# A two-stage attention kernel on one core: batch-wise phases replaced by a pipeline over row tiles

## The chip, the core and the metric

The kernel runs on one core of one Trainium2 chip. The core has five engines with instruction streams of their own: TensorE (PE) for matmuls, VectorE (DVE), ScalarE (ACT), GpSimd (POOL) and SyncE (SP), which here issues all DMA transfers. PE writes to PSUM, eight banks of 2 KB per partition; DVE and ACT read it. Everything else lies in SBUF. The metric is the time of one execution in microseconds; lower is better.

## The reference

q, k and v have 4 batches, 8 heads, 768 positions and 64 dimensions. The first stage is an attention in which a row sees the 8 first (global) keys and the 96 keys up to its own (local):

```python
keep = (pos[None, :] < n_global) | ((rel >= 0) & (rel < n_local))
scores = scale * q @ k.T - slopes * dist          # per head
a = softmax(where(keep, scores, -1e9)); x = a @ v
```

Its result, 4 x 768 x 512, goes into four causal attention experts of width 64, of which each row uses the two with the largest gate logits:

```python
q, k, v = x @ wq[e], x @ wk[e], x @ wv[e]
ye = softmax(causal(scale * q @ k.T)) @ v @ wo[e]
out += weight_of_expert_e(x @ w_gate) * ye        # two experts per row
```

## The kernel before, in words

Rows are worked on in tiles of 128; a batch has 6 of them, and there are 4 batches. Three functions are called per batch. `load_batch` loads q, k and v of a batch (three 1.5-MB transfers, smaller ones for the first batch), POOL casts them to fp16 (L211, L223), and PE transposes q and k by head pair (L215, tile `tp`), which DVE copies out of PSUM (L218). `local_attention` computes, per head pair and two key tiles, the bias and the scores (L256 to L268, tile `sps`), exponentials on ACT into `abuf` (L273, L278), then per row tile the values (L288 to L298, tile `zps`), the division on DVE (L302, L304) and the transposes of the result x (L308, L312). `experts` projects a whole batch at once: k and q with matmuls of 384 columns (L346, tile `pps`), v and gate logits per row tile (L356, `vps`); then the choice of two experts (`top_two`), the causal scores in chunks of up to 512 columns (L385) with exponentials (L392) and masks on POOL (L402), and per row tile values (L410), division (L414 to L418), transposes (L422), output matmul (L429, `ops`), copy on ACT (L432) and store (L433).

The matmuls of a head or an expert have 64 rows; those of an even and an odd one lie on the two halves of the PE array. Three PSUM pools have two buffers each: `psS` (two banks per buffer) for scores, `psZ` for values, and `psT` (one bank) shared by all else: `tp`, `xps`, `pps`, `vps`, `ztps`, `ops`. A scheduler orders each engine's instructions from the program's order, its own cost model and the free buffers; the order is then fixed, and each engine takes its instructions strictly in it. At the end a small test of the softmax sums decides whether a slow general path is run; with these inputs it is not.

## Time and profile before

| | |
|---|---|
| runs | 242.56 us median of 3 (238.79 to 244.24) |
| profiled execution | 238.55 us, its span 236.3 us |
| granted PE clock, mean | 0.937 of full speed |
| instructions | 4,629, of them 1,830 matmuls and as many weight loads |
| one weight load (L410, before values) | 101 ns mean |
| transferred | 27.70 MB, 117 GB/s over the span |
| DMA issues | q, k, v 21, weights 5, global values 16, output 24 |

The profile is of one execution. Its page gives each engine's busy time; the chain of waits follows what released what, back from the end; the timeline shows single instructions, neighbours of one kind merged; the windows give busy time by stretch, with the granted clock. Matmul lengths include their run through the array and overlap, so a matmul's length is no measure of how often one can start. The transferred bytes include 27.34 MB in the kernel's own queue; the rest is instructions.

### The profile page before, as it was taken

How to read it: one execution, taken by the hardware profiler on the slowest of the kernel's cores; microseconds unless marked ns; L12 is line 12 of the kernel's file. 1: busy time of each engine (PE TensorE's matmuls, PEld its weight loads, DVE VectorE, ACT ScalarE, POOL GpSimd, SP SyncE). 2: the span in 40 equal slices, each digit the busy share in tenths (PEclk: the TensorE clock that was granted, in tenths of full speed). 3: DMA queues.
4: the chain of work that ended last, by engine and by line, in shares of the span. 5: the costliest groups of instructions: out<-in, count | busy, mean ns of one | idle time of the engine just before them, and what ended most of it. 6: DMA issues, size and time to landing. Idle time of an engine off the chain costs nothing.

```text
span 236.3 us, 4629 instructions
## 1 busy us (share of the span) xinstructions
PE 183.5 (78%) x1830; PEld 101.0 (43%) x1830; DVE 118.5 (50%) x396; ACT 99.2 (42%) x141; POOL 77.6 (33%) x170
## 2 busy tenths in 40 slices
PE   0656698666987999678969999779868997996770
PEld 0222245543442644555434544654425445543430
DVE  7310114854674532787672612887754216867440
ACT  2112444000058687400278398000595792027840
POOL 8542441195643245249045300080142000002400
PEclk9999959977997999999995899999999999999995
DMA  8999697979799492495990420000002300000032
GB/s 156 218 218 208 122 230 160 210 167 225 189 220 181 138 217 94 144 219 133 219 186 12 154 108 0 3 1 3 0 1 92 152 28 0 3 0 0 37 143 101
DMA packets 43356, 27.70 MB, mean 117 GB/s; under 512 B 26176, under 2 KB 40000, under 8 KB 43328
## 3 DMA queue, kind: packets, MB, share of 16 engines
q1 hardware_dynamic: 43328, 27.34, 51.5%
q8 instruction: 16, 0.26, 0.5%
q14 instruction: 12, 0.10, 0.1%
HBM read 21.05 MB, written 6.29 MB: 116 GB/s over the span
## 4 chain that ended last, share of the span: by engine, by line
PE 59%; DVE 13%; ACT 9%; POOL 7%; issue 4%; DMA 4%; SPq 0%; ACTq 0%; POOLq 0%
PE pps L346 10%; PE sps L256 6%; PE sps L268 6%; PE vps L356 5%; PE ops L429 5%; PE sps L385 5%; POOL s L211 5%; PE zps L410 4%; DVE x L304 3%; PE xps L308 3%; ACT a L392 3%; PE tp L215 3%; DMA vf<-in_v_dram 3%; ACT abuf L273 2%; PE zps L298 2%
## 5 line engine op out<-in xcount | busy, mean ns | idle before, releaser
L392 ACT ACTIVATE a<-sps 128x1024 f16<-128x1024 f32 x40 | 38.9, 1026 | 87.1 <-PE sps L385 87.1
L402 POOL TENSOR_SCALAR_AFFINE_SELECT a<-a 128x256 f16<-128x256 f16 x40 | 16.3, 407 | 74.9 <-ACT a L392 74.9
L273 ACT ACTIVATE abuf<-sps 128x892 f16<-128x892 f32 x32 | 28.7, 920 | 28.4 <-PE sps L268 27.9
L385 PE MATMUL sps<-qT,kT 64*128 64x512 f16 (+3 forms) x128 | 22.2, 329 | 7.2 <-ACT a L392 7.1
L215 PE MATMUL tp<-ident,s 128*128 128x128 f16 x192 | 20.0, 256 | 9.3 <-POOL s L211 8.1
L302 DVE RECIPROCAL rinv<-zps 128x4 f32<-128x4 f32 x48 | 8.3, 177 | 33.7 <-PE zps L298 33.7
L256 PE MATMUL sps<-biasT,ident 128*128 128x446 f16 x64 | 20.3, 398 | 4.3 <-ACT abuf L278 2.1
L215 PEld LDWEIGHTS <-s 128*128 128x128 f16 x192 | 14.5, 114 | 19.8 <-POOL s L211 17.1
L218 DVE COPY kT<-tp 128x768 f16<-128x768 f16 x16 | 8.9, 556 | 24.0 <-PE tp L215 23.9
L308 PE MATMUL xps<-ident,x 128*128 128x128 f16 x96 | 13.3, 223 | 9.1 <-DVE x L304 8.8
L268 PE MATMUL sps<-qT,kT 64*128 64x223 f16 x192 | 19.9, 273 | 0.0
L304 DVE TENSOR_TENSOR x<-zps,rinv 128x256 f16<-128x256 f32 x48 | 19.1, 416 | 1.0 <-PE xps L308 0.2
L211 POOL CAST s<-qf 128x768 f16<-128x768 f32 x16 | 13.2, 825 | 17.5 <-PE tp L215 17.5
L298 PE MATMUL zps<-v,abuf 128*128 128x65 f16 x192 | 18.9, 195 | 0.0
L410 PE MATMUL zps<-v,a 128*128 128x65 f16 x320 | 18.2, 200 | 0.3
L432 ACT ACTIVATE osb<-ops 128x512 f32<-128x512 f32 x24 | 14.0, 608 | 8.1 <-DMA out_dram<-osb 3.5
L410 PEld LDWEIGHTS <-a 128*128 128x128 f16 x320 | 14.5, 101 | 6.0 <-issue 2.3
L295 PE MATMUL zps<-v,abuf 128*128 128x65 f16 x160 | 16.4, 193 | 0.0
L429 PE MATMUL ops<-wo,zt 128*128 128x512 f16 x48 | 15.6, 410 | 0.5 <-DVE n_f L628 0.3
L223 POOL CAST v<-vf 128x768 f16<-128x768 f32 x16 | 12.8, 828 | 7.4 <-DMA vf<-in_v_dram 7.4
L278 ACT ACTIVATE abuf<-sps 128x446 f16<-128x446 f32 (+1 forms) x32 | 13.3, 467 | 4.3 <-PE sps L268 4.3
L211 POOL CAST s<-kf 128x768 f16<-128x768 f32 x16 | 13.2, 824 | 5.7 <-DMA kf<-in_k_dram 5.1
(104 smaller groups left out, 300.4 us busy)
## 6 DMA issues: line engine op xcount, KB each, us to landing
out_dram<-osb SPq DMA_DIRECT2D x24, 256.0 KB
qf<-in_q_dram SPq DMA_DIRECT2D x4, 384.0 KB
kf<-in_k_dram SPq DMA_DIRECT2D x4, 384.0 KB
vf<-in_v_dram SPq DMA_DIRECT2D x4, 384.0 KB
w<-in_moe_wq_dram SPq DMA_DIRECT2D x1, 512.0 KB
w<-in_moe_wk_dram SPq DMA_DIRECT2D x1, 512.0 KB
w<-in_moe_wv_dram SPq DMA_DIRECT2D x1, 512.0 KB
w<-in_moe_wo_dram SPq DMA_DIRECT2D x1, 512.0 KB
```

Of the source, the lines that this page charges most:

```text
L211: G.tensor_copy(s16[:, :, :, :], src[:, 2 * p:2 * p + 2, :, :].rearrange("j h ct d -> j ct h d"))
L215: nc.tensor.transpose(tp[:, ct * P:(ct + 1) * P], s16[:, ct, :, :].rearrange("j h d -> j (h d)"), ident[:, :])
L256: mm(s_ps[:, hh, 0:2 * W].rearrange("r (j n) -> r j n", j=2), lhsT=ident[:, :], rhs=bt.unsqueeze(1).to_broadcast([P, 2, W]), start=True, s ...
L268: mm(s_ps[:, hh, j * W:j * W + ws[j]], lhsT=kT[p][r0:r0 + Dh, ci * P:(ci + 1) * P], rhs=qT[p][r0:r0 + Dh, ci * P:ci * P + ws[j]], start=Fa ...
L273: S_.activation(a[:, :, c0:c0 + 2, 0:W], s_ps[:, :, 0:2 * W].rearrange("r h (j n) -> r h j n", j=2), func=Exp, scale=sc1)
L298: mm(z_ps[:, hq, :], lhsT=a[:, h % 2, ri, 0:P], rhs=v16[:, h, ri, :], start=False, stop=True, skip_group_check=True)
L304: V.tensor_tensor(x16[:, :, :], z_ps[:, :, 0:Dh], rinv.unsqueeze(2).to_broadcast([P, HG, Dh]), op=Alu.mult)
L346: mm(p_ps[:, :], lhsT=w[:, ko, ep, :, :].rearrange("r a d -> r (a d)"), rhs=xT[:, ko, c * HS:(c + 1) * HS], start=(ko == 0), stop=(ko == N ...
L385: mm(s_ps[:, e2, at:at + n * P], lhsT=kT2[r0:r0 + Hd, ep, ci * P:(ci + 1) * P], rhs=qT2[r0:r0 + Hd, ep, q0 * P:(q0 + n) * P], start=first, ...
L392: S_.activation(a2s[ep][:, :, c * 4 * P:c * 4 * P + n_all], s_ps[:, :, 0:n_all], func=Exp, scale=sc2)
L410: mm(z_ps[:, e, :], lhsT=a2(e, ci, ri), rhs=v2[:, ci, e, :], start=(e == 0 and ci == 0), stop=(ci == ri), skip_group_check=True)
L429: mm(o_ps[:, :], lhsT=zt[:, ep, :], rhs=wo16[:, ep, :], start=(ep == 0), stop=(ep == NEP - 1))
```

## The change

The three functions per batch are replaced by six stages per unit, a unit being one row tile of one batch (24 units). A loop over steps calls, in step s, the causal values of unit s-8, the causal scores of unit s-6, the projections of unit s-5, the local values of unit s-4, global scores of three units at a time, the local scores of unit s-1 and the load and transposes of unit s (`prep`). The weights are loaded in step 1. q, k and v come in 256-KB transfers, one each per unit, with four buffers each. Local scores are now computed per row tile over its own and the previous key tile; projections and causal scores have 128 columns per matmul. `top_two` works on 3 row tiles instead of 6. The PSUM pools and the general path are the same.

```diff
+    raw = fast.enter_context(tc.tile_pool(name="raw", bufs=4))
+    pp = fast.enter_context(tc.tile_pool(name="pp", bufs=3))
...
+    NA = 4
...
+    def prep(u):
+        b, ri = divmod(u, NT)
+        f = {}
+        for nm, src in (("k", k), ("q", q), ("v", v)):
+            f[nm] = raw.tile([P, H, Dh], F32, name=nm + "f")
+            dma(f[nm][:, :, :],
+                src[b, :, ri * P:(ri + 1) * P, :].rearrange("h j d -> j h d"))
+        tp = psT.tile([P, 2, NP, P], F16, name="tp", tag="t")
+        for i, nm in enumerate("kq"):
+            s16 = pp.tile([P, H, Dh], F16, name="s16", tag="s16", bufs=4)
+            G.tensor_copy(s16[:, :, :], f[nm][:, :, :])
             for p in range(NP):
+                nc.tensor.transpose(tp[:, i, p, :],
+                                    s16[:, 2 * p:2 * p + 2, :].rearrange("j h d -> j (h d)"),
+                                    ident[:, :])
+        qk[u] = pp.tile([P, 2, NP, P], F16, name="qkT", bufs=7)
+        V.tensor_copy(qk[u][:, :, :, :], tp[:, :, :, :])
...
+        for t in range(NH):
+            for p in range(NP):
+                mm(g_ps[32 * p:32 * p + 32, t * P:(t + 1) * P],
+                   lhsT=kg[:, p, :, :].rearrange("r a g -> r (a g)"),
+                   rhs=qk[u0 + t][:, 1, p, :], start=(r0 != 0 and t == 0),
...
+        for g in range(NP // 2):
+            s_ps = psS.tile([P, 2, 2, 2 * P], F32, name="sps", tag="s")
+            for hh in range(2):
+                flat = s_ps[:, hh, :, :].rearrange("r a n -> r (a n)")
+                mm(flat[:, 0:2 * w].rearrange("r (a n) -> r a n", a=2),
+                   lhsT=ident[:, :], rhs=biasT[:, hh, 2 * g:2 * g + 2, 0:w],
+                   start=True, stop=False, skip_group_check=True)
+            for i in range(2):
+                p = 2 * g + i
+                for prev in range(2 if ri else 1):
+                    n = NL - 1 if prev else P
+                    at = i * w + prev * P
                     for hh in range(2):
+                        r = slice(hh * Dh, hh * Dh + Dh)
+                        mm(s_ps[:, hh, :, :].rearrange("r a n -> r (a n)")[:, at:at + n],
+                           lhsT=qk[u - prev][r, 0, p, :], rhs=qk[u][r, 1, p, 0:n],
                            start=False, stop=True, skip_group_check=True)
...
+            S_.activation(a[:, :, 2 * g:2 * g + 2, 0:w],
+                          s_ps[:, :, :, :].rearrange("r h a n -> r h (a n)")[:, :, 0:2 * w]
+                          .rearrange("r h (a n) -> r h a n", a=2), func=Exp, scale=sc1)
...
+        x_ps = psT.tile([P, NK, P], F16, name="xps", tag="t")
+        for hf in range(2):
+            z_ps = psZ.tile([P, HG, VW], F32, name="zps", tag="z")
+            mm(z_ps[:, :, :], lhsT=ag[:, c:c + P], rhs=vg[:, hf * HG:(hf + 1) * HG, :],
+               start=True, stop=False, skip_group_check=True)
+            for hq in range(HG):
+                h = hf * HG + hq
+                for prev in range(2 if ri else 1):
+                    mm(z_ps[:, hq, :], lhsT=a[:, h % 2, h // 2, prev * P:(prev + 1) * P],
+                       rhs=vs[u - prev][:, h, :], start=False, stop=True,
...
+    def project(u):
+        b, ri = divmod(u, NT)
+        xT = xTs[u]
+        p_ps = psT.tile([P, 2, NEP, P], F32, name="pps", tag="t")
+        for i, w in enumerate((wk16, wq16)):
+            for ep in range(NEP):
+                for ko in range(NK):
+                    mm(p_ps[:, i, ep, :], lhsT=w[:, ko, ep, :, :].rearrange("r a d -> r (a d)"),
+                       rhs=xT[:, ko, :], start=(i == 0 and ep == 0 and ko == 0),
+                       stop=(ko == NK - 1), skip_group_check=True)
...
+        v_ps = psT.tile([P, E * Hd + E], F32, name="vps", tag="t")
+        for ko in range(NK):
+            mm(v_ps[:, :], lhsT=xT[:, ko, :], rhs=wvg16[:, ko, :],
+               start=(ko == 0), stop=(ko == NK - 1))
...
+        if ri % NH == NH - 1:
+            g = u // NH
+            wts[g] = pp.tile([P, NH, E], F32, name="wt")
+            top_two(pp, lgs[g], wts[g], "", NH)
...
+        b, ri = divmod(u, NT)
+        n = ri + 1
+        a2 = a2s[u] = pp.tile([P, 2, NEP * NT, P], F16, name="a2")
+        blocks = [(ep, ci) for ep in range(NEP) for ci in range(n)]
+        for c0 in range(0, len(blocks), 4):
+            part = blocks[c0:c0 + 4]
+            s_ps = psS.tile([P, 2, 4, P], F32, name="cps", tag="s")
+            for i, (ep, ci) in enumerate(part):
+                for e2 in range(2):
+                    r = slice(e2 * Hd, e2 * Hd + Hd)
+                    mm(s_ps[:, e2, i, :], lhsT=k2s[b * NT + ci][r, 0, ep, :],
+                       rhs=q2s[u][r, 1, ep, :], start=(i == 0), stop=True,
+                       skip_group_check=True)
+            S_.activation(a2[:, :, c0:c0 + len(part), :], s_ps[:, :, 0:len(part), :],
+                          func=Exp, scale=sc2)
+        for e2 in range(2):
+            d = a2[:, e2, 0:NEP * n, :].rearrange("r (p c) q -> r p c q", p=NEP)[:, :, ri, :]
+            G.affine_select(out=d, in_=d, pattern=[[0, NEP], [1, P]],
+                            channel_multiplier=-1, base=0, compare_op=Alu.is_ge, fill=0.0)
...
+        z_ps = psZ.tile([P, E, VW], F32, name="zps", tag="z")
+        for e in range(E):
+            for ci in range(n):
+                mm(z_ps[:, e, :], lhsT=a2[:, e % 2, (e // 2) * n + ci, :],
+                   rhs=v2s[b * NT + ci][:, e, :], start=(e == 0 and ci == 0), stop=True,
+                   skip_group_check=True)
...
-    t = load_batch(0)
-    load_weights()
-    for b in range(B):
-        xT = local_attention(b, t)
-        if b + 1 < B:
-            t = load_batch(b + 1)
-        experts(b, xT)
+    L_SCORES, L_GLOBAL, L_VALUES, L_PROJECT, L_CSCORES, L_CVALUES = 1, 3, 4, 5, 6, 8
+    for s in range(NU + L_CVALUES):
+        for lag, stage in ((L_CVALUES, causal_values), (L_CSCORES, causal_scores),
+                           (L_PROJECT, project), (L_VALUES, local_values)):
+            if 0 <= s - lag < NU:
+                stage(s - lag)
+        if s >= L_GLOBAL and (s - L_GLOBAL) % NH == 0 and (s - L_GLOBAL) < NU:
+            global_scores((s - L_GLOBAL) // NH)
+        if 0 <= s - L_SCORES < NU:
+            local_scores(s - L_SCORES)
+        if s < NU:
+            prep(s)
+        if s == 1:
+            load_weights()
```

On PE, at the end of one batch's projections, the order before goes from `pps` to `vps`, with the first causal scores between them:

```order
L346 MATMUL pps<-xT,wq_121 128x384
L346 LDWEIGHTS wq_121
L385 LDWEIGHTS kT_2305
L385 MATMUL sps<-qT_2304,kT_2305 128x512
L356 LDWEIGHTS xT
L356 MATMUL vps<-wvg_123,xT 128x260
```

In the changed kernel, in the middle of the run, the values of one unit (`zps`, from buffers of earlier units) are followed by the output matmul of another and the projections of a third:

```order
L343 LDWEIGHTS a_1003
L343 MATMUL zps<-v_586,a_1003 128x65
L343 MATMUL zps<-v_734,a_1003 128x65
L362 LDWEIGHTS zt
L362 MATMUL ops<-wo_129,zt 128x512
L293 LDWEIGHTS wk_127
L293 MATMUL pps<-xT,wk_127 128x128
```

So neighbours on PE now belong to different units. On SP the order before has the loads of the last batch, then the remaining outputs (the row with x14):

```order
L433 DMA out_dram<-osb 128x512 x2
L192 DMA vf<-in_v_dram 128x48x64
L192 DMA kf<-in_k_dram 128x48x64
L192 DMA qf<-in_q_dram 128x48x64
L198 DMA vgf<-in_v_dram 16x1x64 x2
L433 DMA out_dram<-osb 128x512 x2
L198 DMA vgf<-in_v_dram 16x1x64 x2
L433 DMA out_dram<-osb 128x512 x14
```

The changed order has three loads of later units between two output stores:

```order
L177 DMA qf<-in_q_dram 128x8x64
L177 DMA vf<-in_v_dram 128x8x64
L197 DMA vgf<-in_v_dram 16x1x64 x4
L177 DMA kf<-in_k_dram 128x8x64
L366 DMA out_dram<-osb 128x512
L177 DMA qf<-in_q_dram 128x8x64
L177 DMA vf<-in_v_dram 128x8x64
L177 DMA kf<-in_k_dram 128x8x64
L177 DMA qf<-in_q_dram 128x8x64
L366 DMA out_dram<-osb 128x512
L177 DMA vf<-in_v_dram 128x8x64
```

Each store of `osb` now has loads queued behind it. On DVE the order before copies all `pps` of a batch and then the `vps`:

```order
L218 COPY kT<-tp 128x768
L218 COPY qT<-tp 128x768
L349 CAST kT_1521<-pps 128x384 x2
L349 CAST qT_1520<-pps 128x384 x2
L358 CAST v_1570<-vps 128x4x64
L360 COPY lg<-vps 128x4
```

In the changed order one unit's copies out of the shared `psT` tiles stand between division steps of other units:

```order
L297 CAST kq_3099<-pps 128x512
L305 CAST v_3106<-vps 128x4x64
L308 COPY lg<-vps 128x4
L283 COPY xT<-xps 128x512
L188 COPY qkT<-tp 128x1024
L347 RECIPROCAL rinv_125<-zps 128x4
L349 TENSOR_TENSOR ce<-rinv_125,wt 128x4
L351 TENSOR_TENSOR zs<-zps,ce 128x256
L359 COPY zt<-ztps 128x256
L274 RECIPROCAL rinv_124<-zps 128x4
L276 TENSOR_TENSOR x_3318<-zps,rinv_124 128x256
```

One round of these rows is one unit's share of DVE's work, apart from the choice of experts.

## Rows read from the trace of the kernel before

**Rows 1.** The page, busy us of each engine, share, instructions.
```profile
PE 183.5 (78%) x1830; PEld 101.0 (43%) x1830; DVE 118.5 (50%) x396; ACT 99.2 (42%) x141; POOL 77.6 (33%) x170
```

**Rows 2.** Timeline of PE: start, length in us, engine, line, operation, count merged.
```profile
108.27 0.51 PE L215 MATMUL tp<-ident,s 128*128 128x128 f16 x6 [0.26 <-POOL s L211]
108.72 1.51 PE L346 MATMUL pps<-xT,wk 128*128 128x384 f16 x8
...
190.48 0.54 PE L256 MATMUL sps<-biasT,ident 128*128 128x446 f16 x2
190.96 0.37 PE L268 MATMUL sps<-qT,kT 64*128 64x223 f16 x4
191.26 0.56 PE L256 MATMUL sps<-biasT,ident 128*128 128x446 f16 x2
...
225.22 0.49 PE L410 MATMUL zps<-v,a 128*128 128x65 f16 x11
```

**Rows 3.** Chain of waits: start, length in us, what; first projections of each batch.
```profile
57.31 5.48 PE pps L346 x24
...
108.77 4.38 PE pps L346 x24
...
159.11 4.38 PE pps L346 x24
...
204.03 3.87 PE pps L346 x20
```

**Rows 4.** Windows: busy us of PE, PEld, DVE, ACT, POOL; clock, DMA share, GB/s.
```profile
7.00:57.00 50.00, 34.16 (x309) 19.52 (x309) 16.55 (x43) 11.39 (x17) 23.17 (x49) 0.89 1.02 193
10.00:20.00 10.00, 5.66 (x33) 2.50 (x33) 1.11 (x2) 2.65 (x4) 4.20 (x6) 1.00 1.35 218
57.00:69.50 12.50, 12.50 (x72) 6.25 (x71) 7.78 (x21) 2.18 (x3) 6.08 (x10) 0.89 0.92 208
69.50:80.00 10.50, 7.97 (x82) 3.50 (x82) 5.33 (x26) 9.42 (x13) 4.26 (x13) 0.84 0.67 136
80.00:101.00 21.00, 18.86 (x236) 10.57 (x236) 9.17 (x31) 12.58 (x21) 7.01 (x12) 1.00 0.62 172
101.00:108.70 7.70, 5.42 (x80) 4.17 (x77) 6.29 (x15) 0.00 (x0) 4.90 (x9) 1.00 0.72 148
119.80:131.00 11.20, 8.67 (x80) 4.05 (x79) 5.40 (x25) 9.34 (x12) 5.56 (x12) 0.71 0.45 108
```

**Rows 5.** Waits: who waited for whom, us in total, times, longest.
```profile
ACT a L392 <- PE sps L385: 87.1, 15, 26.2
...
PE sps L385 <- ACT a L392: 7.1, 12, 0.6
```

**Rows 6.** Instructions by line and shape: count, busy us, mean ns, idle before.
```profile
L392 ACT ACTIVATE a<-sps 128x1024 f16<-128x1024 f32 x40 | 38.9, 1026 | 87.1 <-PE sps L385 87.1
L273 ACT ACTIVATE abuf<-sps 128x892 f16<-128x892 f32 x32 | 28.7, 920 | 28.4 <-PE sps L268 27.9
...
L211 POOL CAST s<-qf 128x768 f16<-128x768 f32 x16 | 13.2, 825 | 17.5 <-PE tp L215 17.5
...
L349 DVE CAST qT<-pps 128x384 f16<-128x384 f32 x16 | 8.9, 557 | 3.8 <-PE pps L346 3.0
L218 DVE COPY qT<-tp 128x768 f16<-128x768 f16 x16 | 8.9, 557 | 5.7 <-PE tp L215 5.1
...
L331 DVE TENSOR_TENSOR el<-el,ge 128x24 f32<-128x24 f32 x4 | 1.5, 366 | 2.2 <-ACT el L330 2.2
...
L322 DVE TENSOR_TENSOR ge<-lg,m 128x24 f32<-128x24 f32 x4 | 0.6, 158 | 0.0
```

**Rows 7.** Timeline, the last microseconds.
```profile
226.00 4.62 SPq L433 DMA_DIRECT2D out_dram<-osb  x4
...
229.37 0.60 ACT L432 ACTIVATE osb<-ops 128x512 f32<-128x512 f32 x1 [0.69 <-PE ops L429]
```

**Rows 8.** Waits of SyncE's DMA queue.
```profile
SPq L433 <- ACT osb L432: 119.9, 18, 39.2
```

More of the change, by code (lines that the diff above doesn't have):

```diff
@@ L47 @@
     WP = 2 * P
+    NU = B * NT
+    NH = 3
+    HG = H // 2
     VW = Dh + 1
@@ new lines, in global_scores @@
+    def global_scores(g):
+        u0 = g * NH
+        b, r0 = divmod(u0, NT)
+        kg, _ = gl[b]
+        g_ps = psS.tile([P, NH * P], F32, name="gps", tag="s")
+        if r0 == 0:
+            mm(g_ps[:, 0:P], lhsT=ident[:, :], rhs=gmask[:, :], start=True, stop=False,
+               skip_group_check=True)
+        for t in range(NH):
+            for p in range(NP):
+                mm(g_ps[32 * p:32 * p + 32, t * P:(t + 1) * P],
+                   lhsT=kg[:, p, :, :].rearrange("r a g -> r (a g)"),
+                   rhs=qk[u0 + t][:, 1, p, :], start=(r0 != 0 and t == 0),
+                   stop=True, skip_group_check=True, tile_position=(0, 32 * p))
+        ag = pp.tile([P, NH * P], F16, name="ag", bufs=3)
+        S_.activation(ag[:, :], g_ps[:, :], func=Exp, bias=gbias[:, :], scale=sc1)
+        ags[g] = ag
@@ new lines, in local_scores @@
+    def local_scores(u):
+        ri = u % NT
+        a = abuf[u % NA]
+        w = W if ri else P
+        for g in range(NP // 2):
[10 more added lines that the diff above has]
+                    at = i * w + prev * P
@@ L313, in local_attention, with local_values @@
-        return xT
-    def top_two(pool, lg, wt, nm):
+            S_.activation(a[:, :, 2 * g:2 * g + 2, 0:w],
+                          s_ps[:, :, :, :].rearrange("r h a n -> r h (a n)")[:, :, 0:2 * w]
+                          .rearrange("r h (a n) -> r h a n", a=2), func=Exp, scale=sc1)
+    def local_values(u):
+        b, ri = divmod(u, NT)
+        a, ag, vg = abuf[u % NA], ags[u // NH], gl[b][1]
+        c = (ri % NH) * P
+        x_ps = psT.tile([P, NK, P], F16, name="xps", tag="t")
[8 more added lines that the diff above has]
+                       rhs=vs[u - prev][:, h, :], start=False, stop=True,
+                       skip_group_check=True)
+            rinv = rinv1[:, b, ri, hf * HG:(hf + 1) * HG]
+            V.reciprocal(rinv, z_ps[:, :, Dh])
+            x16 = pp.tile([P, HG, Dh], F16, name="x16")
+            V.tensor_tensor(x16[:, :, :], z_ps[:, :, 0:Dh],
+                            rinv.unsqueeze(2).to_broadcast([P, HG, Dh]), op=Alu.mult)
+            for j in range(2):
+                nc.tensor.transpose(x_ps[:, 2 * hf + j, :],
+                                    x16[:, 2 * j:2 * j + 2, :].rearrange("r h d -> r (h d)"),
+                                    ident[:, :])
+        xTs[u] = pp.tile([P, NK, P], F16, name="xT")
+        V.tensor_copy(xTs[u][:, :, :], x_ps[:, :, :])
@@ new lines, in causal_values @@
+    def causal_values(u):
+        b, ri = divmod(u, NT)
+        n, a2 = ri + 1, a2s[u]
+        z_ps = psZ.tile([P, E, VW], F32, name="zps", tag="z")
[3 more added lines that the diff above has]
+                   rhs=v2s[b * NT + ci][:, e, :], start=(e == 0 and ci == 0), stop=True,
+                   skip_group_check=True)
+        rinv = rinv2[:, b, ri, :]
+        V.reciprocal(rinv, z_ps[:, :, Hd])
+        ce = pp.tile([P, E], F32, name="ce")
+        V.tensor_mul(ce[:, :], rinv, wts[u // NH][:, ri % NH, :])
+        zs = pp.tile([P, E, Hd], F16, name="zs")
+        V.tensor_tensor(zs[:, :, :], z_ps[:, :, 0:Hd],
+                        ce[:, :].unsqueeze(2).to_broadcast([P, E, Hd]), op=Alu.mult)
+        zt_ps = psT.tile([P, NEP, P], F16, name="ztps", tag="t")
+        for ep in range(NEP):
+            nc.tensor.transpose(zt_ps[:, ep, :],
+                                zs[:, 2 * ep:2 * ep + 2, :].rearrange("r e d -> r (e d)"),
+                                ident[:, :])
+        zt = pp.tile([P, NEP, P], F16, name="zt")
+        V.tensor_copy(zt[:, :, :], zt_ps[:, :, :])
+        o_ps = psT.tile([P, D], F32, name="ops", tag="t")
+        for ep in range(NEP):
+            mm(o_ps[:, :], lhsT=zt[:, ep, :], rhs=wo16[:, ep, :],
+               start=(ep == 0), stop=(ep == NEP - 1))
+        o_sb = pp.tile([P, D], F32, name="osb")
+        S_.activation(o_sb[:, :], o_ps[:, :], func=Copy)
+        dma(out[b, ri * P:(ri + 1) * P, :], o_sb[:, :])
@@ L331, in top_two @@
         V.tensor_mul(el[:, :, :], el[:, :, :], ge[:, :, :])
-        z = pool.tile([P, NT], F32, name=nm + "z")
+        z = pool.tile([P, n], F32, name=nm + "z")
         V.reduce_sum(z[:, :], el[:, :, :], axis=Ax.X)
```

310 lines of the change are left out of this document (56 added, 254 removed).

## The prediction

> **What bounds the kernel now.** I read the busy totals first [rows 1]: TensorE (PE) is busy 183.5 of 236.3 us, no other engine over 118.5. So PE is the engine to watch, but a PE that waits between overlapping matmuls also counts as busy, so the next question is what it needs when nothing holds it up.
>
> The timeline of PE answers that [rows 2]. Six transposes of 128 columns with a weight load each take 0.51 us; the last lasts about 0.22, so starts are 58 ns apart. Eight matmuls of 384 columns are (1.51-0.35)/7 = 166 ns apart, eleven of 65 columns (0.49-0.19)/10 = 30 ns. That is 0.43 to 0.46 ns per column whatever the width, with the weight load hidden in every case. Matmuls on 64 rows run in pairs: four of 223 columns end in 0.37 us, of which 0.26 is the last one's own length, so the second pair starts 0.105 us after the first. A change between full-array matmuls and pairs costs more: from the first 446-column bias matmul at 190.48 to the first pair at 190.96 are 0.48 us for 892 columns, which stream in 0.385; from that pair to the next bias matmul are 0.30 us for two pairs (0.21). I take 0.095 us per change.
>
> The program before has 283,600 columns (pairs counted once, the four 32-column strips of the global scores once) and 215 such changes: 283,600 x 0.43 ns = 122 us, plus 20, is 142 us of PE need, 35.5 us per batch. The chain of waits shows the projections of the batches starting at 57.31, 108.77, 159.11 and 204.03 us [rows 3]: a batch takes some 50 us. PE thus uses 0.71 of a batch's time, and the first 57 us serve one batch's first attention only.
>
> Where the rest goes is in the stretches [rows 4]. In the projections (57 to 69.5) PE is never idle, while ScalarE (ACT) works 2.18 of 12.5 us. In the causal scores (69.5 to 80) ACT works 9.42 of 10.5 and PE waits for it. Around the last local values (101 to 108.7) VectorE (DVE) works 6.29 of 7.7 and ACT nothing. In the local scores mixed with causal values (80 to 101) all three have something, and PE is busy 18.86 of 21. ACT's first causal exponentials wait 87.1 us in all for PE, while PE waits 7.1 for ACT [rows 5]: each engine in turn is the limit while the others stand still.
>
> **The change, part by part.** *PE.* The same columns. Projections go from 128 matmuls of 384 columns to 384 of 128, global scores from 32 to 96, local scores from 192 to 352, causal scores from 128 to 336: 656 matmuls and weight loads more, and the instruction order has 226 changes of kind. By the spacing above, 3 x 58 = 174 ns stand for one 166: 128 x 8 ns = 1 us; the others the same or less. With 11 more changes (1 us) PE needs 144 us, 6.0 per unit of 128 rows (24 units). The Trainium skill ("TensorE: Matmul & The Clock Gate", Back-to-back issue gap) gives about 81 ns for sustained matmuls of 128 columns with their weight loads; by it the 384 projections would cost 9 us more, and the total below would be 9 us higher. The transposes at 58 ns speak against it here, so the sum keeps 58.
>
> *DVE.* Copies out of PSUM: 80 before (768 columns in 0.557 us, 384 fp32 in 0.557 [rows 6]), 72 after over the same elements; at most the same time. The choice of two experts is now made 8 times instead of 4, ten instructions of 0.16 to 0.37 us each [rows 6]: 40 more, some 8 us. 118.5 + 8 = 126 us, 5.3 per unit. *ACT:* the same elements; causal exponentials go from 44 to 48 (4 of 1.03 us fewer, 8 half ones more), local ones from 64 to 48 at up to 0.92 [rows 6], global ones and the small ones 4 more each: 99.2 becomes about 102, 4.3 per unit. *GpSimd (POOL):* casts 32 of 0.824 us become 48 over the same elements; with their fixed parts under 90 us, 3.7 per unit. *Transfers:* the same bytes, 0.79 MB in and 0.26 out per unit. The best stretch of only loads moved 218 GB/s [rows 4], so 4.8 us per unit. No engine but PE exceeds 5.3, and in a steady state all work on different units at once.
>
> *Start.* The first output matmul stands in PE's order behind the transposes of 8 units. These need 8 x 0.786 + 2.13 MB of weights = 8.4 MB. At 218 GB/s that is 38.5 us, at the 193 of the stretch 7 to 57, which has the weight loads and their waits for casts in it [rows 4], 43.5; I take 42, near the row with the same kind of traffic. PE's need for everything ahead of this point is 24 us, so loads set it; in the kernel before, only a part of one batch's local attention was done by then.
>
> *Steady part.* PE still needs 144-24 = 120 us. How much of the time will it use? The lower end is 0.73, what the last full period before gives: 44.9 us from 159.11 to 204.03 with a need of 32.8, as it has no loads to transpose. The upper end is 0.90, the mixed stretch 80 to 101, PE busy 18.86 of 21 [rows 4]. The new order is a mixture throughout, but DVE is loaded to 0.72 in it (5.3/6.0 x 0.82) against 0.44 in that stretch, with ACT at 0.6 in both. I take 0.82, midway: 146 us. Ends: 133 and 164.
>
> *Drain.* The last unit's chain from its projection on (three exponentials of 1.03, masks, values, division, output) is about 10 us, and PE has older units' work for part of it: between 0 and 10, I take 5. *Tail.* From the end of the last output copy at 229.97 to the span's end are 6.3 us [rows 7], unchanged. The profiled execution took 238.55, 2.25 outside the span.
>
> Sum: 42 + 146 + 5 + 6.3 + 2.25 = 201.6, taken as **201 us**, against 238.55 for the profiled execution and a median of 242.56 (238.79 to 244.24). What I cost at nothing: extra weight loads (hidden by the matmul ahead; uncovered, the 0.1 us length of each would make 66 us), extra POOL instructions (hidden while POOL is below 6 us per unit).
>
> *Queues passed.* SyncE issues loads and stores in one order. Before, it waits 119.9 us for output copies with nothing behind them that matters [rows 8]. Now loads of later units stand behind each output store: at the first store 8.7 units' loads are issued and the ninth unit's transposes follow soon after, so there a late copy delays a load; at the eleventh store loads are 21 units ahead, three more than are needed, and a delay costs nothing. The few early units may add 3 us each, inside the 0.73 to 0.90.
>
> **Rivals.** (1) *The waits move.* Six tiles per unit (transposes, x, two projections, two output tiles) share two PSUM banks, and each is freed by DVE or ACT. Their own production and copying add to some 7.3 us per unit (0.51+0.7, 1.1+0.4, 0.9+0.7, 0.6+0.6, 0.6, 1.2), 3.7 with two banks; if every reader comes about 1.6 us late, because it queues behind 1-us exponentials or a chain of small DVE instructions, it is 8.4 us per unit, as now. For it: the two are loaded to 0.7 and 0.6 and take their work in a fixed order. Against: between a tile's last matmul and the next use of its bank the new order has another stage. 120/6 = 20 units' work at 8.4 = 168: 42+168+5+8.6 = 224 us, spread 212 to 236.
>
> (2) *Slower: PE drops to 1.2 GHz.* In 119.8 to 131, where PE waited for ACT (busy 9.34 of 11.2 us) between causal pairs, the granted clock was 0.71, in 7 to 57 it was 0.89, in 80 to 101 it was 1.00 [rows 4]. If the steady part has that broken rhythm, its 101 us of streaming can double. Slower than 243.3 (2% over 238.55) needs 40 us more, so 0.4 of the work at the low clock; with 0.6 of it the time is 262. For it: thinner matmuls with many short waits. Against: the mixed stretch kept the full clock at 0.9 busy, and this is the busier kind. The Trainium skill (the same page, A second HAM failure mode) says that a PE made idle again and again by cycling PSUM tiles swings between the two levels; the 0.71 stretch agrees, the mixed one does not.
>
> (3) *Transfers become the bound.* With 256-KB loads and stores alternating, if the rate falls to 130 GB/s, 27.3 MB take 210 us, and with start and tail 222; at 120, 238: no change. For it: loads are requested only as buffers come free. Against: the same packets moved at 208 and 218 GB/s [rows 4], and four units of buffers cover more than 20 us.
>
> **How the numbers follow.** Main case, PE paced: 0.62, 182 to 212. Rival 1: 0.22. Rival 2: 0.09, of it 0.07 slower. Rival 3: 0.07, half of it within 2%. The likeliest gives 201. The range 180 to 228 holds the main case and most of rival 1, and leaves out about 2 in 10. A measurement of this kernel tells about 2% from no change. Faster: 0.62 + 0.20 + 0.04 = 0.86; within 2%: 0.07; slower: 0.07.
>
> **What would show it.** Right: the first output matmul near 42 us; PE busy near 0.9 from then to 185 us without stretches in which ACT or DVE stands still; DVE about 126, ACT about 102 us; PE spacing of 58 ns in the projections; granted clock at 1.00 after the start. Wrong: PE waits for copies of the shared PSUM tiles in every unit (rival 1); long stretches at 0.5 clock (rival 2); casts that wait for loads late in the run (rival 3); projections at 81 ns or more per matmul; a first output matmul after 50 us.

## The result, and the profile after

The changed kernel takes 205.84 us (median of 4 runs, 204.39 to 206.3), against 240.87 for the kernel before in the same comparison: a ratio of 0.861, 95% interval 0.855 to 0.867. The forecast was 201, with 180 to 228 as its range. The profiled execution took 204.39 us, of which the span is 202.7. Some executions, most of them of the kernel before, take over 1.5% longer than its fastest, and ratios here and below leave them out.

The busy totals, answering to [rows 1]: PE's share rises from 78 to 83%. With 656 more matmuls its 168.2 us are still less than the 183.5 before, since time in which PE waits between overlapping matmuls, or streams at a lower clock, counts as busy, and there is less of it (mean granted clock 0.962, before 0.937).

```profile
PE 168.2 (83%) x2486; PEld 116.5 (57%) x2486; DVE 117.0 (58%) x428; ACT 101.9 (50%) x137; POOL 78.5 (39%) x217
```

Five stretches, with the columns of [rows 4]: length, busy us of PE, PEld, DVE, ACT and POOL with counts, clock, DMA share, GB/s.

```profile
0.00:10.00 10.00, 3.49 (x27) 2.16 (x28) 6.09 (x29) 2.37 (x3) 7.29 (x37) 1.00 0.96 180
10.00:36.00 26.00, 17.43 (x185) 9.94 (x184) 7.29 (x21) 5.87 (x7) 13.54 (x44) 0.96 0.94 185
36.00:53.00 17.00, 14.71 (x211) 10.64 (x208) 9.45 (x34) 8.27 (x12) 8.93 (x21) 0.86 0.79 141
53.00:190.00 137.00, 127.91 (x2039) 91.23 (x2035) 91.30 (x333) 82.76 (x112) 47.96 (x116) 1.00 0.57 131
190.00:202.70 12.70, 4.62 (x38) 2.50 (x38) 2.86 (x15) 2.63 (x4) 0.77 (x2) 0.67 0.20 69
```

From 53 to 190 us the mixture is what the forecast hoped for: PE busy 127.91 of 137, DVE at 0.67 and ACT at 0.60 beside it, full clock. The start is where the time is: until 36 us PE is busy 20.9 of 36 us. The output matmuls are one line; its record gives the first and last start:

```profile
L362 PE MATMUL ops<-wo,zt x48: 378/379/632, 53.1 to 196.2; 128*128 128x512 f16 x48
```

53.1 us is 11 later than the forecast's 42. The chain of waits (start, length, what) shows what stands before it:

```profile
10.48 4.66 DMA w<-in_moe_wq_dram
...
15.20 1.33 POOL wq L136 x4
...
16.65 4.34 DMA w<-in_moe_wk_dram
...
21.05 1.44 POOL wk L136 x4
...
22.51 4.44 DMA w<-in_moe_wv_dram
...
27.00 1.44 POOL wvg L141 x4
...
28.86 4.72 DMA qf<-in_q_dram
...
34.38 0.62 PE tp L184 x4
```

The four weight loads share one staging tile (pool `wst`, `bufs=1`), so each waits for POOL's casts of the one before. On SyncE's queue loads of units 2 to 4 stand between them and wait with them; the q in these lines is unit 4's, behind the fourth weight load (issued at 28.45). I had counted the bytes of the weights, not this alternation.

The waits by engine (total, times, longest), answering to [rows 5, 8]:

```profile
POOL a L333 <- ACT a L329: 52.4, 16, 7.3
ACT abuf L253 <- PE sps L250: 50.1, 29, 7.2
...
ACT a L329 <- PE cps L326: 14.7, 20, 2.2
...
PE ztps L355 <- DVE zs L351: 5.8, 10, 1.2
...
PE sps L240 <- ACT a L329: 1.8, 3, 0.6
...
SPq L366 <- ACT osb L365: 96.1, 24, 8.8
```

ACT's causal exponentials waited 87.1 us for PE before, with a longest of 26.2; now 14.7 and 2.2. PE's own waits are small. SyncE still stands 96.1 us before stores, 24 times, now with loads behind it.

PE's timeline around one unit's projections, to be read as [rows 2]:

```profile
101.02 0.61 PE L293 MATMUL pps<-xT,wk 128*128 128x128 f16 x8
101.47 0.61 PE L293 MATMUL pps<-xT,wq 128*128 128x128 f16 x8
101.92 0.61 PE L301 MATMUL vps<-wvg,xT 128*128 128x260 f16 x4
```

Eight matmuls of 128 columns in 0.45 us are 56 ns each, the forecast's 58.

### The profile page after: what moved, and what is told of

Same layout as the page of the kernel before. It is cut to its first block, busy times and chain, and to the rows that moved or that the text cites. A ratio compares the mean times of both kernels' runs of the same rounds, so it can differ in the third digit from the quotient of the medians.

```text
span 202.7 us, 6148 instructions
## 1 busy us (share of the span) xinstructions
PE 168.2 (83%) x2486; PEld 116.5 (57%) x2486; DVE 117.0 (58%) x428; ACT 101.9 (50%) x137; POOL 78.5 (39%) x217
## 4 chain that ended last, share of the span: by engine, by line
PE 59%; DVE 15%; DMA 9%; SPq 5%; ACT 4%; POOL 3%; issue 2%; ACTq 0%; DVEq 0%; POOLq 0%
PE pps L293 11%; PE sps L240 7%; PE ops L362 6%; PE sps L250 6%; PE vps L301 4%; PE tp L184 4%; DVE qkT L188 4%; PE zps L343 4%; PE cps L326 4%; PE xps L279 4%; SPq L177 3%; PE zps L270 3%; PE ztps L355 3%; DVE zs L351 3%; DMA qf<-in_q_dram 2%; DMA w<-in_moe_wq_dram 2%
## 5 line engine op out<-in xcount | busy, mean ns | idle before, releaser
L253 ACT ACTIVATE abuf<-sps 128x892 f16<-128x892 f32 (+1 forms) x48 | 40.2, 862 | 50.3 <-PE sps L250 50.1
L329 ACT ACTIVATE a<-cps 128x1024 f16<-128x1024 f32 (+1 forms) x48 | 42.2, 915 | 15.5 <-PE cps L326 14.7
L297 DVE CAST kq<-pps 128x512 f16<-128x512 f32 x24 | 16.6, 691 | 32.4 <-PE pps L293 32.4
L240 PE MATMUL sps<-biasT,ident 128*128 128x446 f16 (+1 forms) x96 | 29.3, 375 | 3.9 <-ACT a L329 1.8
L188 DVE COPY qkT<-tp 128x1024 f16<-128x1024 f16 x24 | 16.5, 688 | 23.7 <-PE tp L184 22.8
L184 PE MATMUL tp<-ident,s 128*128 128x128 f16 x192 | 18.3, 235 | 10.5 <-POOL s L182 10.3
L182 POOL CAST s<-kf 128x512 f16<-128x512 f32 x24 | 14.8, 619 | 26.0 <-issue 12.2
L250 PE MATMUL sps<-qkT 64*128 64x128 f16 (+1 forms) x352 | 20.4, 226 | 1.3 <-DVE qkT L188 1.3
L270 PE MATMUL zps<-v,abuf 128*128 128x65 f16 x352 | 20.4, 194 | 0.0
L270 PEld LDWEIGHTS <-abuf 128*128 128x128 f16 x352 | 18.0, 98 | 1.7 <-issue 0.4
L191 POOL CAST v<-vf 128x512 f16<-128x512 f32 x24 | 14.7, 614 | 10.8 <-DMA vf<-in_v_dram 10.7
L182 POOL CAST s<-qf 128x512 f16<-128x512 f32 x24 | 14.8, 616 | 8.3 <-DMA qf<-in_q_dram 8.3
L326 PE MATMUL cps<-kq,kq 64*128 64x128 f16 x240 | 14.8, 219 | 0.8 <-ACT a L329 0.6
L293 PE MATMUL pps<-xT,wq 128*128 128x128 f16 x192 | 15.3, 223 | 0.0
```

The lines of the kernel that those rows point to most:

```text
L182: G.tensor_copy(s16[:, :, :], f[nm][:, :, :])
L184: nc.tensor.transpose(tp[:, i, p, :], s16[:, 2 * p:2 * p + 2, :].rearrange("j h d -> j (h d)"), ident[:, :])
L188: V.tensor_copy(qk[u][:, :, :, :], tp[:, :, :, :])
L240: mm(flat[:, 0:2 * w].rearrange("r (a n) -> r a n", a=2), lhsT=ident[:, :], rhs=biasT[:, hh, 2 * g:2 * g + 2, 0:w], start=True, stop=False ...
L250: mm(s_ps[:, hh, :, :].rearrange("r a n -> r (a n)")[:, at:at + n], lhsT=qk[u - prev][r, 0, p, :], rhs=qk[u][r, 1, p, 0:n], start=False, s ...
L253: S_.activation(a[:, :, 2 * g:2 * g + 2, 0:w], s_ps[:, :, :, :].rearrange("r h a n -> r h (a n)")[:, :, 0:2 * w] .rearrange("r h (a n) -> ...
```

## The experiments

Medians are compared with the changed kernel's 205.84 us, which was timed in the first comparison only. The kernel before spreads more (238.7 to 246.5 us over all comparisons), so ratios to it move by a per cent between comparisons, and a difference of a per cent between two experiments decides little. Where idle time of PE or its need ahead of a point is given, it is worked out from all PE rows of that run, the need at the forecast's prices (0.43 ns per column, 0.095 us per change).

### Where the gain comes from: e_nolag and e_phase

e_nolag drops the lags between a unit's stages; with them goes the order within a step, which now begins with the newest unit (`...` marks lines left out):

```diff
-    L_SCORES, L_GLOBAL, L_VALUES, L_PROJECT, L_CSCORES, L_CVALUES = 1, 3, 4, 5, 6, 8
...
+    for s in range(NU + 4):
         if s < NU:
             prep(s)
+            local_scores(s)
...
+        if 2 <= s < NU + 2:
+            for stage in (local_values, project, causal_scores):
+                stage(s - 2)
+        if s >= 4:
+            causal_values(s - 4)
```

> The lags alone undone: the same stages unit by unit, but a unit's local values, projection and causal scores follow one another in one step, and its causal values two steps later; between them stand only the next units' transposes and local scores. Theory A, the lags are what hides each stage's copy or exponential behind another stage's matmuls: a unit shows about 0.5 (division), 0.4 (copy of x), 0.7 (copy of q and k) and half of the exponentials, some 2 us more per unit: 240 to 260 us. Rival B, the order in which each engine's queue is laid out mixes units by itself, so that the written lags matter little: 205 to 215 us.

Measured 244.86 us (243.65 to 245.51), the kernel before 243.94 beside it (238.72 to 246.1): theory A, and the whole gain is gone. The page's row of granted clock (40 slices, tenths), its busy line, and PE's timeline in one unit:

```profile
PE 180.8 (75%) x2486; PEld 131.4 (54%) x2486; DVE 121.4 (50%) x428; ACT 99.7 (41%) x137; POOL 78.0 (32%) x217
...
PEclk9999999769977999569977999569977899569975
```
```profile
121.12 0.28 PE L326 MATMUL cps<-kq,kq 64*128 64x128 f16 x4
122.37 0.34 PE L326 MATMUL cps<-kq,kq 64*128 64x128 f16 x6 [0.97 <-ACT a L329]
...
123.38 0.54 PE L240 MATMUL sps<-biasT,ident 128*128 128x446 f16 x2 [0.61 <-ACT a L329]
...
124.73 1.03 PE L362 MATMUL ops<-wo,zt 128*128 128x512 f16 x2
...
128.78 0.22 PE L219 MATMUL gps<-gmask,ident 128*128 128x128 f16 x1 [0.81 <-ACT abuf L253]
...
130.06 0.28 PE L265 MATMUL zps<-vg,ag 128*128 128x260 f16 x1 [0.78 <-ACT ag L228]
```

Waits of 0.6 to 1.0 us follow one another, and PE drops to half clock (1.2 GHz) for 3.4 to 10.2 us some 27 us apart, 68.9 us in all against 17.3 in the changed kernel: two output matmuls take 1.03 us here and 0.60 there. Of the 39.2 us of span, 26.6 are idle (span less busy: 61.1 against 34.5) and 12.6 more busy time. Matmuls of 128 columns start 107 ns apart at half clock and 56 at full, 0.4 ns more per column. By that the columns streamed at half clock cost some 22 us here, against 4 in the changed kernel; the 106 changes of kind that this order saves (120 against 226) give part of that back. This is the forecast's rival 2, seen in another kernel: the Trainium skill ("TensorE: Matmul & The Clock Gate", A second HAM failure mode: psum-queue depth-cycling) describes a PE that swings between its levels when short idle times come again and again, and this trace agrees. With the lags the steady part shows none of it (clock 1.00). They have a price, though: without them the first output matmul comes at 43.4 us, 9.6 earlier than in the changed kernel; the loss is in the 191.9 us from the first to the last one, against 143.1.

e_phase keeps the lags and undoes the mixing of batches and of the two attentions (with more buffers for q, k, v and x, as that needs):

```diff
-    for s in range(NU + L_CVALUES): ...
+    for b in range(B):
+        ...                       # global_scores; local_scores, local_values 3 behind
+        for s in range(NT):
+            project(u0 + s)
+        for s in range(NT + 2):   # causal_values 2 behind causal_scores; next batch's prep
+            ...
```

> The mixing alone undone: the same tiles, matmuls, copies and stage functions as in the changed kernel, but a batch at a time (six units of local attention with their own lags, six projections, six units of causal attention with the next batch's transposes among them), with enough buffers for that. Theory A, the gain of the change is that ScalarE's, VectorE's and PE's stages of different units overlap: with phases ACT limits causal scores (48 exponentials, 42 us in all), PE the projections, and each phase drains: 225 to 245 us, PE idle or waiting for ACT a at more than 20 us. Rival B, the gain comes from the smaller tiles and the shorter start (one unit instead of one batch before work begins): 203 to 215 us.

Measured 220.38 us (219.44 to 221.32): between the two, neither theory. The first output matmul starts at 64.5 us, 11.4 later than in the changed kernel, and the batches follow every 45 us (64.5, 109.7, 154.5) where units a batch apart follow every 42 (53.1, 95.3, 136.8). In a whole batch PE is busy 0.90:

```profile
66.00:111.30 45.30, 40.99 (x626) 27.89 (x621) 29.78 (x99) 25.32 (x35) 18.45 (x46) 1.00 0.80 168
```

ACT's causal exponentials wait 42.2 us for PE instead of 14.7, so the engines do take turns more, but lags within a phase already cover most of it. Of the 35 us, then, mixing the phases is worth 14.5. The first output matmul's 11.4 us are only in part a loss: by then PE has done more (a need of 29.8 us against 24.2) and been idle 6.0 us longer (23.4 against 17.4). From the first to the last output matmul it's idle 4.7 us longer (15.6 against 10.9), and the order has 30 changes of kind more. The other 20 us come with thin units and lags inside a phase.

### What sets the start: e_wbuf, e_wlate, e_hoist

```diff
-    wst = fast.enter_context(tc.tile_pool(name="wst", bufs=1))
+    wst = fast.enter_context(tc.tile_pool(name="wst", bufs=4))
```

> One size: the staging tile of the weights gets four buffers instead of one, so that no weight load waits for the casts of the one before. Changed kernel: 205.8 us; in its chain the weight loads stand one behind another (4.66, 4.34, 4.44 us, with 1.33, 1.44, 1.44 us of casts between them), and the first output matmul starts at 53.1 us instead of the 42 forecast. Theory A, the chain of weight loads sets the start: four loads and their casts, 22 us, fall to the 2.1 MB's own 10 to 12 us, the first output matmul comes at 43 to 46 us, 196 to 200 us. Rival B, the start is bound by what the DMA engines carry at this packet size (DMA share 0.94 and 185 GB/s from 10 to 36 us): the first output matmul stays at 50 us or later, 203 to 206 us.

Measured 202.29 us (201.99 to 204.44), ratio 0.845 (0.838 to 0.852); first output matmul at 50.4 us. Between the two: loads went from 185 to 217 GB/s, so rival B's limit isn't one, yet the start is B's, since PE stood from 16.9 to 23.1 us: unit 2's q and v were still behind 2.1 MB of weights. PE's idle time before the first output matmul is 17.4 us, as in the changed kernel. What is shorter is its busy time, 33.0 against 35.7 us, with none at half clock where the changed kernel has 6.8 us. So the gain may be the clock's and not the load rate's; no run separates them.

```profile
10.00:36.00 26.00, 16.50 (x196) 10.35 (x195) 7.20 (x19) 6.28 (x8) 14.05 (x41) 1.00 1.18 217
```
```profile
23.11 0.61 PE L184 MATMUL tp<-ident,s 128*128 128x128 f16 x4 [6.17 <-POOL s L182]
```

e_wlate, on top of e_wbuf, moves the weights two units further down:

```diff
-        if s == 1:
+        if s == 3:
             load_weights()
```

> Two places: four staging buffers for the weights as in e_wbuf, and their loads and casts three units into the program (behind unit 3's loads and casts) instead of one. In e_wbuf the first output matmul came at 50.4 us: unit 2's loads stood behind 2.1 MB of weights and PE was idle from 16.9 to 23.1 us, then needed 27 us to get there. Theory A, the 24 us of PE work ahead of the first output matmul stand in series with that wait, and loads by themselves (8.4 MB at the 217 GB/s of e_wbuf, 39 us) do not set it: with the weights behind four units PE works while they land, first output matmul at 42 to 46 us, total 194 to 198 us. Rival B, the projections of unit 0 now wait for weights that come later, and the start stays at 49 to 52 us: 201 to 204 us.

Measured 203.63 us (202.83 to 204.41), first output matmul at 52.2: theory A fell as stated, but rival B's reason was not the one at work either. POOL's timeline shows it:

```profile
24.58 0.13 POOL L190 MEMSET v<- 128x8 f16 x1 [5.30 <-PE zps L270]
27.03 0.13 POOL L190 MEMSET v<- 128x8 f16 x1 [2.32 <-PE zps L270]
27.07 1.43 POOL L136 CAST wq<-w 128x256 f16<-128x256 f32 x4
...
32.32 0.61 POOL L182 CAST s<-kf 128x512 f16<-128x512 f32 x1
```

The MEMSETs of units 7 and 8, placed early in POOL's order, waited for PE to release the v tiles of units 0 and 1, and the weights' casts stood behind them. e_hoist takes away what makes them wait:

```diff
-        vs[u] = pp.tile([P, H, VW], F16, name="v16", bufs=7)
-        G.memset(vs[u][:, :, Dh:VW], 1.0)
+        vs[u] = vbuf[u % NV]      # ring of seven, column of ones set once ahead
```

> One place, on top of e_wlate: the v tiles become a ring of seven buffers whose column of ones is set once, instead of a MEMSET per unit. In e_wlate's trace the MEMSETs of the 7th and 8th next unit stood ahead of the weights' casts on POOL and waited 5.30 and 2.32 us for PE to release unit 0's and 1's tiles, and the casts of unit 4 came only at 32.3 us, with PE idle for 5.46 us. Theory A, POOL's order set that start: all weights have landed by some 26 us, unit 4's first cast comes at 27 to 28 us, first output matmul at 44 to 48 instead of 52.2 us, 196 to 200 us. Rival B, the weights land too late anyway or PE's order holds the start: first output matmul at 50 us or later, 202 to 205 us.

Measured 200.85 us (200.21 to 202.38), ratio 0.837 (0.832 to 0.842); first output matmul at 49.0, just above A's 44 to 48, the total just above its 200. Theory A in its mechanism: the first cast of unit 4 comes at 29.22 instead of 32.32, now waiting for its load alone, and PE's idle time before the first output matmul falls from 17.1 us in e_wlate to 13.6.

```profile
29.22 0.61 POOL L189 CAST s<-kf 128x512 f16<-128x512 f32 x1 [0.25 <-DMA kf<-in_k_dram]
```

One number nearly recurs: from the transposes of unit 4's q, which stands behind weight loads in all of these, to the first output matmul are 53.1 - 34.4 = 18.7 us in the changed kernel, 17.0 in e_wbuf (from 33.4), 17.9 in e_wlate (34.3) and in e_hoist (31.1), for 12.3 to 13.9 us of need. Loads and POOL's order decide when this piece begins (in e_wbuf by way of the long wait at unit 2), PE's work and its clock how long it is: in e_best below it is 21.5 us, 11.3 of them at half clock.

### The price of PE's instructions: e_split and e_group

```diff
-                    mm(p_ps[:, i, ep, :], lhsT=w..., rhs=xT[:, ko, :], ...)
+                    for c in (0, Hd):
+                        mm(p_ps[:, i, ep, c:c + Hd], lhsT=w..., rhs=xT[:, ko, c:c + Hd], ...)
```

> One cost doubled: each of the 384 projection matmuls of 128 columns becomes two of 64 columns with the same weights, 384 matmuls and weight loads more for the same columns. Theory A, a matmul costs its columns (0.43 ns each, 30 ns for the 65 columns of the values) and weight loads are hidden: 0 to 2 us more, 205 to 208 us. Rival B, a matmul with a new weight load has a floor: at the 56 ns of the 128-column ones it is 384 x 56 = 21 us of PE, 222 to 228 us; at the 98 ns of a weight load over 250 us.

Measured 208.09 us (206.98 to 209.71): 2.3 us more, at the edge of A and far from B.

```profile
111.48 0.64 PE L294 MATMUL pps<-xT,wk 128*128 128x64 f16 x16
111.96 0.63 PE L294 MATMUL pps<-xT,wq 128*128 128x64 f16 x16
```

Sixteen matmuls of 64 columns take 0.48 us, eight of 128 took 0.45: 0.03 x 48 such groups is 1.4 us, and weight loads stay hidden at 30 ns a matmul. The forecast's 1 us for its added matmuls stands. The 9 us that it worked out from the Trainium skill's figure for 128 columns ("TensorE: Matmul & The Clock Gate", Back-to-back issue gap) does not show: those matmuls run 56 ns apart here.

e_group emits the bias matmuls of both halves of the local scores before the pairs:

```diff
+        tiles = []
         for g in range(NP // 2):
             s_ps = psS.tile(...)
+            tiles.append(s_ps)
             ...                   # the two bias matmuls
+        for g, s_ps in enumerate(tiles):
             for i in range(2):    # the pairs, the exponential
```

> One part of the order: in the local scores of a unit the bias matmuls of both halves come first and then all pairs, so that PE changes between full-array and 64-row matmuls 48 times less; the work is the same. Theory A, each such change costs 0.095 us of PE, and PE sets the pace: 48 x 0.095 = 4.6 us, at 0.85 use about 5 us less, 200 to 202 us. Rival B, the change costs nothing by itself (the time is the drain of one shape's array use, given back elsewhere) or PE does not set the pace: 204.5 to 206.5 us. Rival C, both tiles of local scores must now be free together before the first pair, and PE waits for the exponentials: 207 to 212 us, with PE's waits for ACT a and abuf grown from 2 to over 10 us.

Measured 204.06 us (203.47 to 204.84), ratio 0.851 (0.845 to 0.856): 1.8 us less, between A and B. The built order changes kind 196 times instead of 226, not 48 times less, so A's own price gives 30 x 0.095 = 3 us. Inconclusive between a part of A and nothing. The price itself can be read from the changed kernel's records: over its 85 changes into pairs and 85 out of them between 53 and 188 us, start to start beyond the columns (0.43 ns each) is 99 and 106 ns on average (worked out from all PE rows of the stretch). The two matmuls of a pair start 3 to 4 ns apart and stream together, so the columns of one are subtracted in full; the 127 ns in e_pool4's expectation below count half of them. The forecast took 95 for both. The Trainium skill ("TensorEngine Tiling (Array Packing)", Key Properties) says that a change of tiling mode drains the engine; that each change costs about 100 ns here agrees.

### Banks and queues: e_psT3, e_pool4, e_order, e_storeq

```diff
-    psZ = ...(tc.tile_pool(name="psZ", bufs=2, space=PSUM))
-    psT = ...(tc.tile_pool(name="psT", bufs=2, space=PSUM))
+    psZ = ...(tc.tile_pool(name="psZ", bufs=1, space=PSUM))
+    psT = ...(tc.tile_pool(name="psT", bufs=3, space=PSUM))
```

> One size: the six tiles per unit that share two PSUM banks get three, and the two kinds of value tiles that shared two get one. Theory A, neither of them paces the kernel as PE's own work does, but one bank of value tiles puts the division (0.42 us and a reciprocal of 0.09) between the halves of the local values: up to 3 x 0.6 us per unit that other work of PE, standing behind in order, can't fill: 215 to 235 us. Rival B, the forecast's rival 1, the two shared banks are what holds the kernel at 0.85 of PE's need: a third bank gives 5 to 12 us, 194 to 201 us. Rival C, neither matters: 204 to 207 us.

Measured 213.97 us (212.01 to 214.8), ratio 0.890 (0.878 to 0.901): A in its sign, a little under its size. PE's wait for the causal division grows from 5.8 to 16.3 us (the reciprocal in it takes 0.17 us, not the 0.09 of the expectation):

```profile
PE ztps L355 <- DVE zs L351: 16.3, 18, 2.5
```

e_pool4 lets all eight kinds share four banks (`bufs=4`, `psT = psZ`, one tag):

> One allocation: the eight kinds of tiles that use two pools of two PSUM banks each (transposes, x, projections, output; and the two value tiles) share one pool of four. Transitions of PE between full-array and row- or column-tiled matmuls fall from 226 to 182, since tiles are then handed out in one order. Theory A, PE's own work paces the steady part (busy 127.9 of 137 us from 53 to 190) and a transition costs 0.11 us (in the trace of the changed kernel 85 into pairs at 97 ns and 85 out of them at 127 ns beyond the columns): 44 x 0.11 = 5 us less, 200 to 202 us. Rival B, the banks pace it (the forecast's first rival): four banks for any tile give more than that, 192 to 198 us, and the 5.8 us of waits for the x and zs tiles go. Rival C, a value tile now waits behind another stage's tile in the common order: PE's waits for DVE grow from 8 to over 15 us, 207 to 216 us.

Measured 225.89 us (224.5 to 226.43), ratio 0.939 (0.934 to 0.944): C, and beyond its range. From 53 to 190 us PE is busy 117.5 of 137 at a clock of 0.97, and its waits for DVE have grown:

```profile
PE ztps L355 <- DVE zs L351: 10.9, 12, 1.2
...
PE xps L279 <- DVE x L276: 9.6, 19, 1.3
PE ops L362 <- DVE zt L359: 4.0, 11, 0.4
```

Half clock adds some 7 us (0.4 ns for each column streamed at it is 10.3 us, 3.6 in the changed kernel). The 44 changes of kind fewer are paid for many times over. My reading, not tried by itself: with two pools PE's built order can take a stage forward past another, while one pool hands tiles out in program order, and PE waits where it had interleaved. e_order, on top of it and with e_group's order, has 150 changes:

```diff
+        if 0 <= s - L_CSCORES < NU:
+            causal_scores(s - L_CSCORES)
+        if 0 <= s - L_SCORES < NU:
+            local_scores(s - L_SCORES)
+        if 0 <= s - L_PROJECT < NU:
+            project(s - L_PROJECT)
...
```

> The order of stages within a step, on top of e_pool4's common pool and e_group's two bias matmuls first: local scores come right behind causal scores. Transitions of PE fall from 226 to 150, the work is the same. Theory A, as in e_pool4: 76 x 0.11 = 8.4 us less, 196 to 199 us. Rival B, the five score tiles of a unit now come close together on two buffers, and PE stands before them until ScalarE has made exponentials (0.9 to 1.0 us each): PE's waits for ACT grow from 5 to 15 us or more, 203 to 215 us.

Measured 225.12 us (224.46 to 228.47), ratio 0.935 (0.930 to 0.941): worse than either theory and no different from e_pool4, whose loss it carries. B's mechanism shows little (PE's waits for ACT at the score tiles: 4.9 us), and the 32 changes fewer bought nothing beside PE's waits for DVE. What the order would do without the common pool was not run.

```diff
-        dma(out[b, ri * P:(ri + 1) * P, :], o_sb[:, :])
+        nc.scalar.dma_start(out[b, ri * P:(ri + 1) * P, :], o_sb[:, :])
```

> One queue: the output stores are issued on ACT's queue behind the copy they wait for, and no longer on SyncE's queue ahead of loads. SyncE waited 96 us for output copies in the changed kernel, 8.8 us of it at the first store, with the loads of unit 8 and later behind it. Theory A, those waits delay the early units (about 3 us each for two or three of them): 197 to 202 us, first store's wait gone and the idle time of casts waiting for loads of q, k, v cut from 28 us to under 15. Rival B, four units of buffers cover it, and issuing costs ACT some 0.4 us per store on an engine that is half idle: 204 to 207 us.

Measured 204.96 us (204.69 to 207.51), ratio 0.857 (0.849 to 0.866): rival B. Loads from 36 to 53 us ran at 205 GB/s instead of 141, and POOL's waits for loads of q, k and v fell from 28.5 to 4.5 us, as theory A asked, but nothing came earlier for it (first output matmul at 53.2). In this profile PE has 17.1 us of half clock before that matmul, against 6.8, so a small gain in the start could be hidden.

### The best of them: e_best

e_hoist with e_group's order, and the output weights loaded at `s == 4`:

> On top of e_hoist (200.85 us): the output weights, which the first output matmul alone needs, are loaded and cast one unit later, behind unit 4; and the bias matmuls of both halves of the local scores come first, as in e_group. PE's transitions fall from 234 to 197. Theory A, both terms count: unit 4's first cast waits for 0.5 MB less (29.2 us becomes 26 to 27), and 37 transitions less at 0.11 us are 4 us, of which e_group showed 1 to 2 for 30: 195 to 199 us. Rival B, loads set that start in any order (8.4 MB at 213 to 217 GB/s, 39 us, plus 8 to 10 us from the last transposes to the first output matmul), and the transitions are covered by other waits: 199.5 to 202 us.

Measured 201.34 us (199.49 to 202.64), ratio 0.822 (0.817 to 0.826, with the kernel before at 244.34 in that comparison): rival B, no different from e_hoist's 200.85. Unit 4's first cast came at 28.25 instead of 29.22, A's 26 to 27 not reached: on POOL it follows the casts of the other weights without a pause, and those of wv had waited 2.00 us for their load. In its profile PE ran at half clock from 27.9 to 41.6 us and the first output matmul came at 51.8; from it to the start of the last one are 141.8 us, against 142.9 in e_hoist. e_hoist has the lowest median, 2.4% under the changed kernel; e_best's lower ratio comes from a slower kernel before beside it, and the two aren't told apart.

## Why the prediction held, step by step

- **Start, 42 us: the step that failed.** Measured 53.1, 11 us too late, past the 50 that the forecast named as a sign against it. "PE's need for everything ahead of this point is 24 us, so loads set it" took the larger of two terms that lie partly in series: the last 17 to 19 us before the first output matmul begin only when unit 4, behind the weights, has come. Until 53.1 us PE is idle 17.4 us and busy 35.7, so neither term alone is the time. Taking 3.5 us of the idle time away brought the first output matmul 3.2 us forward (e_hoist against e_wlate). The busy part is itself far over the need of 24: the 6.8 us of half clock make some 2 us of that by their columns, the rest is not split up here. On top, loads ran at 185 GB/s, as the weights' one staging tile let only one of them run at a time; four tiles gave 217 and a median 3.5 us lower, but the same idle time (e_wbuf).
- **Steady part and drain, 146 + 5 us.** From 53.1 to the end of the last output copy at 197.25 are 144.2 us: 7 less. The columns streamed between 53 and 190 are 0.81 of the program's, 116 of the 144 us of need in 137 us: 0.85 where the forecast chose 0.82 between 0.73 and 0.90. The choice between the two bounds held.
- **PE's need.** 56 ns spacing (58 forecast), 99 and 106 ns a change (95): confirmed, the second forecast a little low.
- **DVE 126, ACT 102.** ACT 101.9. DVE 117.0, 9 below: summed over all its records DVE's time did grow, from 130.9 to 135.3 us (the choice of two experts from 8.6 to 14.8, copies less), but the page counts time once where one record begins before the last has ended, and that happens more now (18.3 us against 12.4). With half the elements seven of the ten instructions of the choice are shorter, but three are longer. Of those in [rows 6], L331's 366 ns became the 170 of L384, and L322's 158 the 242 of L375:

```profile
L375 DVE TENSOR_TENSOR ge<-lg,m 128x12 f32<-128x12 f32 x8 | 1.9, 242 | 0.1
...
L384 DVE TENSOR_TENSOR el<-el,ge 128x12 f32<-128x12 f32 x8 | 1.4, 170 | 1.0 <-ACT el L383 0.2
```

- **Tail and outside, 8.55 us.** The chain ends as in [rows 7]:

```profile
195.97 0.61 PE ops L362 x2
...
196.65 0.60 ACT osb L365
```

  202.7 - 197.25 = 5.45, and 204.39 - 202.7 = 1.69: 7.1. So the sum of 201.6 against 204.4 rests on errors of +11.1, -6.8 and -1.4 that partly cancel; the nearness is luck, and better than the steps.
- **Queues passed.** Costed inside the range at up to 3 us for a few units: no gain clear of the spread when it was taken away (e_storeq).
- **Rival 1, banks.** Didn't come: PE's waits at the shared tiles are 5.8 us or less. The thin units are close to it, though: one bank less for the value tiles costs 8 us, one common pool 20. Three banks for the shared tiles beside two for the values were not run.
- **Rival 2, clock.** Not in the steady part (1.00), but 6.8 us of half clock at 33.8 to 40.6 in the start; fully there without lags (e_nolag). **Rival 3, transfers.** 131 GB/s in the steady part were asked for, not the limit: after 53 us POOL's casts waited 24.5 us for q, k and v, but PE's 10.3 us of waiting for casts lie ahead of it.

## What to carry to other kernels

When every engine takes its turn as the limit, put each stage of a unit a stage-time behind its producer; here it was the lag, not the thin unit by itself, that paid: without it PE waited in short pieces and ran four times as long at half clock. The lag also lengthens the start (53.1 us with, 43.4 without). For a pipeline's start, add the work that the last arrival still has before it; don't take the larger of load time and work. Before giving tiles a common pool or moving an operation up a queue, see what the built order then puts behind it.

## What the runs showed that I had not expected

- With one staging tile a weight load of 512 KB took 4.34 to 4.66 us, 112 to 121 GB/s for itself, with loads of the units issued beside it; from 10 to 36 us all loads together ran at 185 GB/s, with four staging tiles at 217.
- Half clock in the start follows no single wait: around a wait of 1.88 us (changed kernel) PE had 6.8 us at 1.2 GHz, around one of 2.69 us (e_best) 13.7, around one of 6.17 us (e_wbuf) none.
- Fewer changes of tiling did not go with a shorter time: 150 instead of 226 with a time 19 us longer (e_order, with the common pool), 120 with one 39 us longer (e_nolag). PE waited more in both, so the price per change was worth paying for an order that hides waits.
